# Value matmuls of the transposed score groups by Strassen's method, with score tiles in planned slots

## The chip, the cores and the metric

One Trainium2 chip, one core. The metric is the device time of the whole program in microseconds (us), the median of several executions.

The engines: PE (matmuls), PEld (loads of PE's stationary operand, beside PE), DVE, ACT, POOL, and SP, which only issues transfers here. SPq in a view is SP's transfer queue.

## The reference, cut to what matters

Eight batches of 3008 tokens: an attention with squared relu and a gate, then a feed-forward layer with g = h cos h.

```python
scores = (1.0 / S) * np.matmul(z, z.transpose(0, 2, 1))   # z: 3008 x 64, so scores are symmetric
attn = np.maximum(scores, 0.0) ** 2
x = u * np.matmul(attn, v)                                 # u, v: 3008 x 256
# ... cut: the eight batches laid one after the other, 24064 tokens
h = x @ w_in                                               # 256 -> 2048
g = h * np.cos(h)
y = g @ w_out                                              # 2048 -> 256
```

## The kernel before: the parts that matter

A batch is cut into 6 columns of 512 tokens (the last has 448), a column into 4 blocks of 128. The score group (c, R) is the 512 x 512 piece of columns c and R. Only the groups with R >= c are computed; for R > c the DMA makes a transposed copy, which column R uses later.

```python
# s_squares: relu on ACT, square on DVE, then the transposed copy by the DMA (queue of SP)
nc.scalar.activation(rt[:, i, :], banks[k], AF.Relu)
nc.vector.tensor_tensor(
    t.rearrange("p s k w -> p s k w")[:, 2 * p:2 * p + 2], rv, rv, ALU.mult)
if p == 1:
    fresh[(b, c, R)] = [t[:, :, k, :] for k in range(K)]
    if R > c and not direct(b, R, c):
        tt = tpool.tile([P, K, K, P], FP16, name="tt")
        turned[(b, c, R)] = tt
        nc.sync.dma_start_transpose(
            tt.rearrange("p s k w -> p (s k) w"),
            t.rearrange("p s k w -> p (s k w)"))
# ... cut
# av_chunks: a column's 23 full blocks into two PSUM banks, both halves of v
for nh in range(NDH):
    for n in range(n0, n1):
        j = order[n]
        wn, a = moving(j)                    # a fresh block, or one of a transposed copy
        chain(nc.tensor.matmul(
            acc[nh][:, 0:wn],
            vs(b, j // G)[:, j % G, nh * P:(nh + 1) * P], a,
            start=(n == 0), stop=(n == NJ - 2)))
if n1 == NJ - 1:
    finish()                                 # DVE: x = acc * ut, frees the two banks
# ... cut
# h_quantum: what DVE must do in time, for PE's six other PSUM banks to come free
nc.scalar.activation(c16, hp, AF.Sin, bias=pihalf, scale=inv_s2)
nc.vector.tensor_tensor(gs[(m, ft // FG)][:, ft % FG, :], hp, c16, ALU.mult)
```

Everything is an event at a planned time (8 units a column, about 3.2 us each). `chain` fixes PE's order by these times; a scheduler sets the order of the other engines by when it believes operands to be ready. A *visit* is a bundle of score matmuls with their relus and squares, in the midst of feed-forward work; a visit ends with up to two transposes.

## Time and profile before

| | before |
|---|---|
| time, median of 3 | 1247.27 us (1246.61 to 1248.53) |
| span of the profiled run | 1244.6 us |
| PE busy / idle | 1234.4 / 10.2 us |
| granted clock, mean | 1.000 |
| transposed copy, issue to landing (min / median / max) | 4.3 / 5.4 / 17.6 us |

The prediction below shows the lines themselves. Three habits help with all that follows. First the busy line, for who is full. Then the chain that ended last, for whether the full engine also sets the end. Then single stretches of the timeline, where one line is `start, duration, engine, line, operation, output<-inputs, count, [idle before <-releaser]`.

### The profile page before, as it was taken

How to read it: one execution, taken by the hardware profiler on the slowest of the kernel's cores; microseconds unless marked ns; L12 is line 12 of the kernel's file. 1: busy time of each engine (PE TensorE's matmuls, PEld its weight loads, DVE VectorE, ACT ScalarE, POOL GpSimd, SP SyncE). 2: the span in 40 equal slices, each digit the busy share in tenths (PEclk: the TensorE clock that was granted, in tenths of full speed). 3: DMA queues.
4: the chain of work that ended last, by engine and by line, in shares of the span. 5: the costliest groups of instructions: out<-in, count | busy, mean ns of one | idle time of the engine just before them, and what ended most of it. 6: DMA issues, size and time to landing. Idle time of an engine off the chain costs nothing.

```text
span 1244.6 us, 20404 instructions
## 1 busy us (share of the span) xinstructions
PE 1234.4 (99%) x7533; PEld 680.0 (55%) x7533; DVE 782.0 (63%) x1389; ACT 844.7 (68%) x1609; POOL 145.8 (12%) x201
## 2 busy tenths in 40 slices
PE   9899999999999999999999999999999999999998
PEld 3355555555555555555555555555555555555556
DVE  7766666666666666656666566665666656666555
ACT  6666676666676766667766667766667766667646
POOL 3210101001010010100101011011010111100000
PEclk9999999999999999999999999999999999999999
DMA  9997958679576795757958569685695957957311
GB/s 162 152 174 129 141 91 119 114 122 142 99 117 111 117 144 106 115 111 110 149 101 121 107 109 150 101 129 99 109 158 92 129 101 112 152 101 108 72 33 45
DMA packets 484212, 144.85 MB, mean 116 GB/s; under 512 B 432400, under 2 KB 484112, under 8 KB 484112
## 3 DMA queue, kind: packets, MB, share of 16 engines
q1 hardware_dynamic: 356448, 88.73, 43.1%
q0 software_dynamic: 100400, 29.77, 24.7%
q10 hardware_dynamic: 27264, 25.06, 6.3%
q8 instruction: 59, 0.97, 0.3%
q14 instruction: 41, 0.34, 0.1%
HBM read 60.29 MB, written 24.64 MB: 68 GB/s over the span
## 4 chain that ended last, share of the span: by engine, by line
PE 97%; DMA 2%; DVE 0%; ACT 0%; issue 0%; DVEq 0%; ACTq 0%
PE acc L310 37%; PE w L361 26%; PE w L344 26%; PE w L223 6%; DMA tt<-a 1%; DMA ut<-ust_62 1%; PE acc L285 1%; DMA x<-in_z_dram 0%; DVE g L351 0%; PE w L191 0%; DVE x L331 0%; ACT zT_63 L196 0%; ACT rt L256 0%; DVE a L258 0%; DVE zst L186 0%
## 5 line engine op out<-in xcount | busy, mean ns | idle before, releaser
L361 PE MATMUL w<-w_out_71,g 128*128 128x256 f16 x3008 | 448.6, 273 | 0.0
L344 PE MATMUL w<-x,w_in_70 128*128 128x512 f16 x1504 | 445.6, 379 | 0.8 <-DVE g L351 0.8
L361 PEld LDWEIGHTS <-g 128*128 128x128 f16 x3008 | 294.2, 98 | 191.6 <-issue 1.4
L256 ACT ACTIVATE rt<-w 128x512 f16<-128x512 f32 x489 | 253.1, 613 | 121.2 <-PE w L223 121.2
L258 DVE TENSOR_TENSOR a<-rt 128x1024 f16<-128x1024 f16 x254 | 173.8, 691 | 180.8 <-ACT rt L256 178.3
L344 PEld LDWEIGHTS <-w_in_70 128*128 128x128 f16 x1504 | 147.0, 98 | 59.2 <-issue 3.9
L90 POOL DMA_DIRECT2D ust_62<-in_u_dram x64 | 44.7, 704 | 385.8 <-PE acc L310 355.9
L240 ACT ACTIVATE rt<-w 128x512 f16<-128x512 f32 (+3 forms) x176 | 62.8, 449 | 39.7 <-PE w L223 39.7
L331 DVE TENSOR_TENSOR x<-acc,ut 128x64 f16<-128x64 f32 (+7 forms) x178 | 69.6, 431 | 29.1 <-PE acc L310 26.6
L310 PE MATMUL acc<-a,v_65 128*128 128x512 f16 x336 | 85.8, 380 | 0.0
L310 PEld LDWEIGHTS <-v_66 128*128 128x128 f16 x552 | 51.9, 98 | 61.8 <-issue 14.1
L310 PEld LDWEIGHTS <-v_65 128*128 128x128 f16 x552 | 51.6, 98 | 60.0 <-issue 13.1
L310 PEld LDWEIGHTS <-v_67 128*128 128x128 f16 x552 | 51.9, 98 | 58.7 <-issue 11.1
L310 PEld LDWEIGHTS <-v_68 128*128 128x128 f16 x552 | 51.9, 98 | 57.7 <-issue 10.9
L310 PE MATMUL acc<-a,v_66 128*128 128x512 f16 x312 | 79.4, 379 | 2.6 <-DVE x L331 2.6
L310 PE MATMUL acc<-a,v_68 128*128 128x512 f16 x312 | 79.2, 379 | 0.0
L310 PE MATMUL acc<-a,v_67 128*128 128x512 f16 x312 | 79.1, 379 | 0.0
L368 ACT ACTIVATE ob<-w 128x256 f32<-128x256 f32 x188 | 73.0, 388 | 5.3 <-PE w L361 5.3
L241 DVE TENSOR_TENSOR a<-rt 128x512 f16<-128x512 f16 (+3 forms) x176 | 47.3, 321 | 44.0 <-ACT rt L240 44.0
L90 POOL DMA_DIRECT2D ust_61<-in_u_dram x48 | 36.5, 766 | 224.4 <-PE acc L310 206.7
L310 PE MATMUL acc<-tt,v_68 128*128 128x512 f16 (+1 forms) x240 | 62.2, 371 | 0.0
L310 PE MATMUL acc<-tt,v_67 128*128 128x512 f16 (+1 forms) x240 | 62.1, 371 | 0.0
(1546 smaller groups left out, 1399.8 us busy)
## 6 DMA issues: line engine op xcount, KB each, us to landing
out_dram<-ob ACTq DMA_DIRECT2D x92, 256.0 KB, 2.3
ust_61<-in_u_dram POOLq DMA_DIRECT2D x48, 128.0 KB, 4.0
ust_62<-in_u_dram POOLq DMA_DIRECT2D x32, 128.0 KB, 4.4
a<-a SPq DMA_TRANSPOSE x132, 3.0
v_65<-in_v_dram POOLq DMA_DIRECT2D x4, 512.0 KB, 6.1
v_66<-in_v_dram POOLq DMA_DIRECT2D x4, 512.0 KB, 6.6
v_68<-in_v_dram POOLq DMA_DIRECT2D x4, 512.0 KB, 6.2
v_67<-in_v_dram POOLq DMA_DIRECT2D x4, 512.0 KB, 6.2
```

Of the source, the lines that this page charges most:

```text
L90: hold(nc.gpsimd.dma_start(dst, src))
L223: chain(nc.tensor.matmul(sp[:, s0 * P:], zt[h, R * K + k + 1 - lo, :], zt[h, j0 + s0:j0 + K, :].rearrange("p j w -> p (j w)"), start=True, ...
L240: nc.scalar.activation(rt[:, i, k * P:], banks[k][:, k * P:], AF.Relu)
L241: nc.vector.tensor_tensor(t[:, k, k:, :].rearrange("p s w -> p (s w)"), rt[:, i, k * P:], rt[:, i, k * P:], ALU.mult)
L256: nc.scalar.activation(rt[:, i, :], banks[k], AF.Relu)
L258: nc.vector.tensor_tensor(t.rearrange("p s k w -> p k s w")[:, 2 * p:2 * p + 2], rv, rv, ALU.mult)
L285: chain(nc.tensor.matmul(accs[(b, c)][nh], vs(b, NG - 1)[h, G - 1, nh * P:(nh + 1) * P], a[h], start=False, stop=False))
L310: chain(nc.tensor.matmul(acc[nh][:, 0:wn], vs(b, j // G)[:, j % G, nh * P:(nh + 1) * P], a, start=(n == 0), stop=(n == NJ - 2)))
L331: nc.vector.tensor_tensor(x[:, nh, :], acc[nh][:, o:o + n], ut[:, nh, o:o + n], ALU.mult)
L344: chain(nc.tensor.matmul(hp, w_in16[:, k, ft * P:(ft + 1) * P], x[:, k, :], start=(k == 0), stop=(k == NDH - 1)))
L361: chain(nc.tensor.matmul(ys[m][:, 0:D], gs[(m, f4)][:, ft % FG, ts * P:(ts + 1) * P], w_out16[:, ft, :], start=(ft == 0), stop=(ft == NFT ...
L368: nc.scalar.activation(obs[m][:, i, :], ys[m][:, 0:D], AF.Copy, bias=0.0, scale=inv_s2)
```

## The change

Its intent: PE is full, so do fewer columns of matmul. Four transposed blocks times v are a 2 x 2 product of halves, and Strassen's method (in Winograd's form) needs 7 half products for 8. In columns 2 to 5 up to four transposed groups go this way, 102 groups in all. DVE prepares the sums of scores, POOL the sums of v, ACT and DVE combine the products. The first sums overwrite the transposed copy in place, so score tiles get 18 planned slots instead of two rotating pools of 9 and 13.

```diff
+    slots = [kpool.tile([P, K * CW], FP16, name=f"s{i}") for i in range(NSLOT)]   # NSLOT = 18
-    apool = pool("a", 9)
-    tpool = pool("at", 13)
+    spool = pool("sum", 1)
 ...
+    def v_sums(b, R):                       # POOL, four operations a group (first shown)
+        nc.gpsimd.tensor_tensor(o[:, 0], t[:, k1, d2], t[:, k1, d1], ALU.subtract)
 ...
+    def a_sums1(b, c, R):                   # DVE, reads and writes the transposed copy
+        s1 = quarter(b, c, R, 0, 1)
+        nc.vector.tensor_tensor(s1, s1, quarter(b, c, R, 1, 1), ALU.add)
+        nc.vector.tensor_tensor(
+            second(b, c, R), s1, quarter(b, c, R, 0, 0), ALU.subtract)
+    def a_sums2(b, c, R):                   # DVE, 1024 elements
+        nc.vector.tensor_tensor(dst, src, sub, ALU.subtract)
+    def product(b, c, n):                   # PE: two matmuls of half width a group
+            for k in range(2):
+                chain(nc.tensor.matmul(
+                    acc[bank][:, cols], lhs[:, k, :], rhs[:, k, :], ...))
+    def keep(b, c, n):                      # ACT copies products 1, 5, 7; DVE adds
+        if n in (1, 5):
+            nc.scalar.copy(p15[:, n // 5, 0:h], acc[n // 5][:, h:2 * h])
 ...
+                for i, R in enumerate(W):
+                    at(t - 2.5 + 0.5 * i, 2, lambda b=b, c=c, R=R: a_sums1(b, c, R))
+                    at(t + 1.5 + 0.3 * i, 2, lambda b=b, c=c, R=R: a_sums2(b, c, R))
+                for n, o in ((1, 1.0), (5, 1.0), (2, 1.0), (6, 1.4), (7, 3.0), (3, 3.0), (4, 3.4)):
+                    at(t + o, 2, lambda b=b, c=c, n=n: product(b, c, n))
```

## The prediction

> **What bounds the kernel now.** I read the page's first two parts, then the chain of waits, then the costliest groups, then one stretch of the timeline, then the rows of the transposed score tiles.
>
> ```profile
> PE 1234.4 (99%) x7533; PEld 680.0 (55%) x7533; DVE 782.0 (63%) x1389; ACT 844.7 (68%) x1609; POOL 145.8 (12%) x201
> PEclk9999999999999999999999999999999999999999
> PE acc L310 37%; PE w L361 26%; PE w L344 26%; PE w L223 6%; DMA tt<-a 1%; DMA ut<-ust_62 1%; PE acc L285 1%; DMA x<-in_z_dram 0%; DVE g L351 0%; PE w L191 0%; DVE x L331 0%; ACT zT_63 L196 0%; ACT rt L256 0%; DVE a L258 0%; DVE zst L186 0%
> ```
>
> PE is busy 99% at a full clock, and the chain that ended last is PE for 97%: 37% in the value matmuls (L310) that the change rewrites. The next lines ask whether PE is really streaming, and how late ACT, DVE and the transposes come behind it. Columns of the timeline: start, duration, engine, line, operation, count.
>
> ```profile
> 606.15 0.59 PE L344 MATMUL w<-x,w_in_70 128*128 128x512 f16 x2
> 606.58 0.60 PE L361 MATMUL w<-w_out_71,g 128*128 128x256 f16 x4
> 607.02 0.59 PE L344 MATMUL w<-x,w_in_70 128*128 128x512 f16 x2
> ...
> 610.58 0.82 PE L223 MATMUL w<-zT_63 64*128 64x512 f16 x6
> 611.00 3.04 ACT L256 ACTIVATE rt<-w 128x512 f16<-128x512 f32 x6 [1.52 <-PE w L223]
> ...
> 612.84 5.49 SPq L265 DMA_TRANSPOSE tt<-a  x2
> ...
> 613.88 0.73 ACT L348 ACTIVATE c_7345<-w,pihalf 128x512 f16<-128x512 f32 x1
> ...
> 616.24 0.38 ACT L368 ACTIVATE ob<-w 128x256 f32<-128x256 f32 x1
> ```
> ```profile
> DMA to landing us min/median/max: 4.3/5.4/17.6
> ```
>
> Starts: two 512-column matmuls take 0.43 us, four 256-column ones 0.44 us, so PE loses nothing and halving a matmul's width costs almost nothing. There is no waiting to remove: only columns. After a visit of six score matmuls (610.58) ACT needs 3.0 us for its six relus, works through four sines until 616.2 and then the output copy: 6.0 us behind the visit. And a tile that the DMA transposes lands 4.3 us after its issue at best, 5.4 in the median (last fence, the rows of tile tt). Today only PE reads it, much later, so nobody cares.
>
> **What the Trainium skill says.** (1) "TensorE: Matmul & The Clock Gate", section "Wait — 56ns, not 53.3ns?": a matmul takes N/2.4 GHz plus about 2.5 ns. The trace agrees: starts lie 216 ns apart at 512 columns, 109 at 256, 189 at 448. (2) "PSUM — Partial Sum Buffer", section "PSUM bank collisions raise a hardware error": two engines must not touch one bank at once, so an accesses' order must be guarded by bank. The trace of before has no such case; in the built order of after, the copy of product 1 does wait for product 2, which writes the other half of that bank. (3) The same page, "Engine vs sequencer instructions": ScalarE and VectorE queues are strict FIFO. The trace's DVE order is exactly the built order, all 1389 instructions. (4) "VectorE: DVE Perf Modes", section "The perf-mode tier table": 16-bit tensor_tensor runs at two elements a cycle, with a PSUM operand at one. The trace agrees: 691 ns for 1024 elements of L258, 416 ns for 256 from PSUM (L331).
>
> **The change part by part.**
>
> PE. A full transposed group was 4 blocks x 2 halves = 8 matmuls of 512 columns, 8 x 0.2158 = 1.727 us. It becomes 7 products x 2 = 14 of 256, 14 x 0.1092 = 1.528 us: 0.198 saved. In column 5 (448 wide): 8 x 0.1892 - 14 x 0.0958 = 0.172. Groups: columns 2, 3, 4 have 2+3+4 in each of batches 1 to 7, and 3+4 in batch 0: 70; column 5 has 4 x 8 = 32. Saved: 70 x 0.198 + 32 x 0.172 = **19.4 us**. Everything on PE saved would give 1247.3 - 19.4 = 1227.9. That is 1.6%, so a gain over 2% is out of reach.
>
> DVE. Per group two sums of 512 elements (423 ns each, row L241) and one of 1024 (691): 1.54 us, x 102 = 157. Per Strassen column (31 of them) two of 256 from PSUM (0.416) and one of 512 (0.68): 1.5, x 31 = 47. DVE goes from 782 to about 985 us, 79% of the span. ACT: 3 copies of 0.38 x 31 = 35, to 880. POOL: 128 sums of v, in column 0, a column and more before use. None of these becomes a bound by itself. What counts is where PE must wait in order. I counted that in the built order, batch by batch (batches 1 to 7 have the same pattern), against the times above.
>
> - Columns 3 and 4: product 6 follows product 2 with nothing between, and waits for the ACT copy that waits for product 2. Last matmul of product 2 starts at s; ACT starts at s + 0.27 (its duration) + 0.04 (the visit: 610.58 + 0.38, the mean of a 512-column matmul, to 611.00), copies 0.38, PE answers 0.05 later: s + 0.74, where s + 0.11 was due. 0.63 us each, 16 times, and once in column 5 of batch 7, which has no score visit: 17 x 0.63 = **10.7 us**.
> - Column 2: a score visit fills that gap, but product 4 comes due 5.5 us after the visit, and its ACT copy stands behind six relus, four sines and an output copy (6.0 us) + 0.38 + 0.05. 0.9 us, 7 times: **6 us**. In column 5 the products are longer, and it fits.
> - The first activation sums of each group stand in the DVE queue right behind the squares that made the group, because the scheduler moved them far forward of their place in the text. Each needs the transposed tile. DVE blocks until it lands, 4.3 to 5.4 us after the squares (2 us more for the second of a visit), where the next DVE work, the product g, is due 2 to 4 us earlier. PE waits wherever it needs a PSUM bank that a late g, or a late finish of a column, frees. Per batch I find: before column 5 (second of a visit, finish late) 1.0 to 1.3; at the wrap to column 0 (same) 1.4 to 2.0; column 1, where the last score matmul needs the g behind the blocked sum, 0.4 to 1.4; three smaller places, 0.5 to 1.2 together. 3.3 to 5.9 us a batch, x 7 = **23 to 41 us**.
>
> Sum: 1247.3 - 19.4 + 10.7 + 6 + (23 to 41) = 1268 to 1286.
>
> **The rivals.**
>
> *All of the saving arrives* (1228). For it: PE is the bound everywhere, and DVE and ACT have a third of the span free. Against: PE has no idle time to absorb a wait, and the waits of product 6 on ACT are certain in the order. It needs zero cost at 17 + 7 places.
>
> *Only the ACT round trips cost* (1247.3 - 19.4 + 16.7 = 1245, level). This is the case if the six PSUM banks and the buffers let PE run on while DVE is blocked. For it: in the timeline g ends about 1 us before the score matmul that needs its bank, so part of each block is swallowed; and a wait of PE in one place gives DVE time for the next, so my sum counts some twice. Against: the blocks are 2 to 3 us and the slack 1.
>
> *DVE blocked on transposes sets the pace* (1268 to 1286, the sum above). For it: landing times of 4.3 us at best, a strict FIFO, a built order that puts the sum there 13 times a batch. Were the transposes slower under more traffic (maximum 17.6), it would be above 1290.
>
> *The planned slots (18 for 22 buffers) add waits of their own.* The SP and DVE waits on PE in the order are for matmuls long past; I give it nothing.
>
> **Range and chances.** I trust the ACT waits (16.7 us) most, and take the DVE ones at about half of the middle of their range, 32, for the double counting: -19.4 + 16.7 + about 19 = +16, or **1264 us**. The low end, 1232, is all of the saving with a few of the waits; the high end, 1288, is the full sum. Over 2% faster is 1222.8, below what all columns saved can give: 0.01. Over 2% slower begins at 1272.2, inside my sum of the third rival: 0.35. Within 2%: 0.64.
>
> **What will show it.** PE busy time must fall by about 19 us and the value lines must show 1428 matmuls of 224 and 256 columns at 96 and 109 ns from start to start; if these run slower, the first term is wrong. The waits must list PE behind the ACT copies about 24 times, 0.6 to 0.9 us each. DVE must show idle time before the first sums (a_sums1), released by the transposes, some 1 to 3 us each and about 100 times; PE must then show waits on g and on the finish of a column, together 20 to 40 us. If DVE waits there but PE shows no wait on DVE, the second rival holds; if DVE does not wait, my reading of the order is wrong and the time is near 1240. If PE waits for v sums on POOL or for slots, I missed a term.

## The result, and the profile after

**1407.04 us** (median of 4, 1401.65 to 1409.64). The ratio to the kernel before is 1.1278, with a 95% interval of 1.1252 to 1.1304. A ratio here is the mean time of one kernel's fast runs over the mean of the other's fast runs of the same rounds, so it is not quite the ratio of the medians.

From the page of the kernel after: the busy line, PE's busy digits, the granted clock, and the chain by engine.

```profile
PE 1272.8 (90%) x8145; PEld 752.0 (53%) x8145; DVE 955.0 (68%) x1788; ACT 885.3 (63%) x1702; POOL 234.6 (17%) x329
...
PE   6689799997999879998799987999879898899999
...
PEclk8799999998999989999999999999999999999999
...
PE 70%; DMA 16%; DVE 6%; ACT 4%; issue 3%; ACTq 0%; DVEq 0%; SPq 0%
```

PE has fewer columns to do and yet is busy *longer*, 1272.8 for 1234.4 us. It is also idle for 1407.9 - 1272.8 = 135.1 us, where it was 10.2 before. Its busy digits dip to 7 with a rhythm, about every five slices of 35 us: once a batch. The chain that ended last, 97% PE before, now leads for 16% through DMAs. That is the first sign of the cause: not an engine that is full (DVE is at 68%), but transfers that someone stands and waits for.

Next the waits of the kernel after, `engine, output, line <- what ended the wait: total us, times, longest`. L376 is the first sum of a group (the in-place add of `a_sums1`), L458 the product g, L347 the finish of a column, L236 the score matmuls, L419 the Strassen products, L439 and L432 the ACT copies of products.

```profile
DVE s L376 <- DMA s<-s: 199.5, 72, 7.8
...
ACT c L455 <- DVE g L458: 84.9, 57, 7.1
...
PE w L236 <- DVE g L458: 46.8, 17, 7.0
...
PE acc L419 <- DVE x L347: 37.5, 13, 5.3
...
PE acc L324 <- DVE x L347: 10.4, 2, 7.4
...
PE acc L419 <- ACT q L439: 9.4, 14, 0.9
...
PE acc L419 <- ACT p L432: 8.2, 17, 0.8
```

Read it downwards as one chain. DVE stands 199.5 us before the first sums, until a transposed copy lands. Behind it in DVE's queue are g and the finish of a column, so ACT and PE wait for these: PE for 46.8 + 37.5 + 10.4 = 94.7 us. The waits of PE on ACT, which the prediction trusted most, are there too, 31 times, but only 17.6 us together. One more wait is left out here: 12.8 us of PE on a relu of DVE (L267), 8.9 of them in one piece at the start; e2 and e5 come to it.

One such place in the timeline of the kernel after. The visit is at 510 us; the two transposes are issued at 512.44 and 516.5.

```profile
512.44 8.23 SPq L278 DMA_TRANSPOSE s<-s  x2
...
513.68 0.69 DVE L271 TENSOR_TENSOR s<-rt 128x1024 f16<-128x1024 f16 x1 [0.29 <-ACT rt L269]
...
514.29 1.28 DVE L458 TENSOR_TENSOR g<-w,c 128x512 f16<-128x512 f32 x2
...
516.35 0.44 PE L236 MATMUL w<-zT 64*128 64x512 f16 x3
...
520.54 0.94 DVE L376 TENSOR_TENSOR s<-s 128x512 f16<-128x512 f16 x1 [4.98 <-DMA s<-s]
...
521.40 1.27 DVE L458 TENSOR_TENSOR g<-w,c 128x512 f16<-128x512 f32 x2
522.13 1.18 PE L236 MATMUL w<-zT 64*128 64x256 f16 x3 [5.35 <-DVE g L458]
...
524.07 1.06 PE L451 MATMUL w<-x,w_in 128*128 128x512 f16 x2
```

The first copy lands at 520.45, 8.0 us after its issue. Until then DVE does nothing, although sines for g are ready. Six PSUM banks fill up; PE issues three score matmuls and stops. Only after 4.98 us does the sum run, then g, and then PE, which has stood for 5.35 us. The last line holds a second loss: two matmuls of 512 columns take 1.06 us, where the same pair took 0.59 in the kernel before.

Windows of 1 us of the kernel after, with busy time (and instructions) of PE, PEld, DVE, ACT and POOL, then the granted clock, DMA share and GB/s:

```profile
526.00:527.00 1.00, 1.00 (x4) 0.46 (x3) 0.98 (x2) 0.12 (x1) 0.00 (x0) 0.50 1.38 216
527.00:528.00 1.00, 1.00 (x6) 0.55 (x4) 0.40 (x1) 0.56 (x1) 0.00 (x0) 0.66 0.44 86
528.00:529.00 1.00, 1.00 (x9) 0.69 (x8) 0.35 (x2) 0.69 (x1) 0.00 (x0) 1.00 0.00 0
```

From 522 to about 527.7 the clock is 0.50 (the mean of 0.66 in the second window holds both rates), so PE is "busy" and does half the work: a wait of 5.35 us costs about 8, by an estimate from these numbers (5.35 and half of 5.5). The Trainium skill, page "TensorE: Matmul & The Clock Gate", Part 1: The HAM clock gate, says that PE runs at half rate after an idle window of about 3.4 us and returns to full after a window of sustained work. The trace agrees in kind (0.50, then 1.00); its lengths differ, as the last section tells.

This makes the batch from 489.40 to 661.15 us 171.75 us long, where a batch of the kernel before takes about 154.5 (its transposes of one place in the batch start at 568.74 and 723.21). Its PE is idle for 12.8 us: 4.2 and 5.35 in two places behind late copies, 2.0 in three waits on ACT, and small ones.

### The profile page after: what moved, and what is told of

Read it like the earlier page. It is cut to its first block, busy times and chain, and to the rows that moved or that the text cites. A ratio compares the mean times of both kernels' runs of the same rounds, so it can differ in the third digit from the quotient of the medians.

```text
span 1407.9 us, 22304 instructions
## 1 busy us (share of the span) xinstructions
PE 1272.8 (90%) x8145; PEld 752.0 (53%) x8145; DVE 955.0 (68%) x1788; ACT 885.3 (63%) x1702; POOL 234.6 (17%) x329
## 4 chain that ended last, share of the span: by engine, by line
PE 70%; DMA 16%; DVE 6%; ACT 4%; issue 3%; ACTq 0%; DVEq 0%; SPq 0%
PE w L468 18%; PE w L451 18%; PE acc L324 18%; DMA s<-s 16%; PE acc L419 10%; PE w L236 5%; ACT rt L269 2%; DVE g L458 2%; DVE x L347 1%; DVE s L271 1%; DVE s L391 1%; DVE s L376 1%; PE acc L298 1%; ACT c L455 1%; ACT p L432 0%
## 5 line engine op out<-in xcount | busy, mean ns | idle before, releaser
L455 ACT ACTIVATE c<-w,pihalf 128x512 f16<-128x512 f32 x752 | 502.0, 704 | 300.7 <-PE w L451 209.9
L458 DVE TENSOR_TENSOR g<-w,c 128x512 f16<-128x512 f32 x752 | 491.2, 685 | 89.3 <-ACT c L455 86.1
L468 PE MATMUL w<-w_out,g 128*128 128x256 f16 x3008 | 453.1, 274 | 0.0
L451 PE MATMUL w<-x,w_in 128*128 128x512 f16 x1504 | 452.1, 384 | 0.0
L324 PE MATMUL acc<-s,v 128*128 128x512 f16 (+1 forms) x1392 | 345.2, 386 | 10.4 <-DVE x L347 10.4
L271 DVE TENSOR_TENSOR s<-rt 128x1024 f16<-128x1024 f16 x254 | 187.3, 743 | 113.7 <-ACT rt L269 113.5
L324 PEld LDWEIGHTS <-v 128*128 128x128 f16 x1392 | 130.2, 99 | 177.0 <-issue 64.6
L376 DVE TENSOR_TENSOR s<-s 128x512 f16<-128x512 f16 (+1 forms) x102 | 43.7, 429 | 199.6 <-DMA s<-s 199.5
L451 PEld LDWEIGHTS <-w_in 128*128 128x128 f16 x1504 | 149.0, 99 | 52.9 <-issue 6.7
L236 PE MATMUL w<-zT 64*128 64x512 f16 (+3 forms) x684 | 109.9, 374 | 63.3 <-DVE g L458 46.8
L419 PE MATMUL acc<-s,vsum 128*128 128x256 f16 (+1 forms) x816 | 112.5, 279 | 19.5 <-ACT q L439 9.4
L419 PE MATMUL acc<-s,v 128*128 128x256 f16 (+1 forms) x612 | 87.2, 286 | 37.5 <-DVE x L347 37.5
L419 PEld LDWEIGHTS <-vsum 128*128 128x128 f16 x816 | 79.7, 101 | 51.1 <-issue 42.9
L419 PEld LDWEIGHTS <-v 128*128 128x128 f16 x612 | 62.6, 104 | 48.6 <-DVE x L347 37.3
L236 PEld LDWEIGHTS <-zT 64*128 64x128 f16 x684 | 26.0, 95 | 113.3 <-issue 100.6
L347 DVE TENSOR_TENSOR x<-acc,ut 128x64 f16<-128x64 f32 (+7 forms) x178 | 68.9, 431 | 3.6 <-PE acc L324 3.5
```

The costliest lines, as they stand in the source:

```text
L236: chain(nc.tensor.matmul(sp[:, s0 * P:], zt[h, R * K + k + 1 - lo, :], zt[h, j0 + s0:j0 + K, :].rearrange("p j w -> p (j w)"), start=True, ...
L271: nc.vector.tensor_tensor(t.rearrange("p s k w -> p k s w")[:, 2 * p:2 * p + 2], rv, rv, ALU.mult)
L324: chain(nc.tensor.matmul(acc[nh][:, 0:wn], vs(b, j // G)[:, j % G, nh * P:(nh + 1) * P], a, start=(start and n == 0), stop=(last and n == ...
L347: nc.vector.tensor_tensor(x[:, nh, :], acc[nh][:, o:o + n], ut[:, nh, o:o + n], ALU.mult)
L419: chain(nc.tensor.matmul(acc[bank][:, cols], lhs[:, k, :], rhs[:, k, :], start=(n in (1, 5) and i == k == 0), stop=(i == len(W) - 1 and k ...
L451: chain(nc.tensor.matmul(hp, w_in16[:, k, ft * P:(ft + 1) * P], x[:, k, :], start=(k == 0), stop=(k == NDH - 1)))
```

## The experiments

Eleven kernels ran, all correct. "Gain" compares medians.

| kernel | median us | range | ratio to before (95%) |
|---|---|---|---|
| e1: slots alone | 1244.42 | 1243.79 to 1248.26 | 0.9996 (0.9974 to 1.0018) |
| e2: after, first sums late | 1272.33 | 1270.67 to 1273.88 | 1.0217 (1.0193 to 1.0241) |
| e3: before + an early idle sum | 1360.25 | 1358.55 to 1367.41 | 1.0930 (1.0896 to 1.0964) |
| e4: before + a late idle sum | 1266.57 | 1264.77 to 1272.95 | 1.0177 (1.0145 to 1.0208) |
| e5: e2 + sums of v paced | 1254.78 | 1251.44 to 1256.17 | 1.0064 (1.0044 to 1.0085) |
| e6: e5 + products reordered | **1237.41** | 1236.35 to 1238.22 | **0.9931** (0.9914 to 0.9948) |
| e7: e6, first sums early again | 1368.10 | 1365.78 to 1372.09 | 1.0985 (1.0957 to 1.1013) |
| e8: after, 2 of 13 sums late | 1358.16 | 1356.45 to 1362.39 | 1.0900 (1.0875 to 1.0925) |
| e9: after, the other 11 late | 1339.18 | 1335.50 to 1340.90 | 1.0738 (1.0715 to 1.0762) |
| e10: after, 3 of 13 late | 1311.59 | 1309.73 to 1314.73 | 1.0533 (1.0509 to 1.0558) |
| e11: after, one v load later | 1402.43 | 1396.90 to 1405.20 | 1.1238 (1.1208 to 1.1269) |

### e1: the slots alone

```diff
-    NW = 4
+    NW = 0
```

> The changed kernel with Strassen switched off in every column (NW = 0): the planned slots stay, all value matmuls are full ones again. Theory A (the loss is DVE blocked on freshly issued transposes): there are no sums, so the time is that of before, 1247 us within 5, with PE at 99% and a clock of 1.00. Rival C (18 planned slots in place of 22 rotating buffers make score tiles wait): over 1270 us.

Measured 1244.42 us, ratio 0.9996. No Strassen, 18 slots: as fast as before. The slots cost nothing, and the fourth rival is out.

### e2: the first sums behind the last g

The sums stay what they are. Each first sum only gets an order (no wait on a semaphore) behind the last g issued before it in the text, so it stands where its text stands.

```diff
-        nc.vector.tensor_tensor(s1, s1, quarter(b, c, R, 1, 1), ALU.add)
+        add = nc.vector.tensor_tensor(s1, s1, quarter(b, c, R, 1, 1), ALU.add)
+        if lastg:
+            after(add.ins, lastg[0], NOSYNC)
 ...
-        nc.vector.tensor_tensor(gs[(m, ft // FG)][:, ft % FG, :], hp, c16, ALU.mult)
+        g = nc.vector.tensor_tensor(gs[(m, ft // FG)][:, ft % FG, :], hp, c16, ALU.mult)
+        lastg[:] = [g.ins]
```

> The changed kernel, with one thing more: the first activation sum of a group may not be moved ahead of the last g product issued before it in the text, so it stands in the DVE queue where the text has it, a column or more after its transpose was issued. Same work on every engine. Theory A: DVE's 200 us of waiting on transposes ends, PE no longer waits on g or on the finish of a column, the clock is 1.00, and what is left is -19 us of columns and about +17 us of round trips over ACT: 1240 to 1255 us. Rival B (the amount of new work on DVE and ACT, or the ACT round trips, set the pace): over 1340 us.

Measured 1272.33 us: 134.7 us come back, for an order alone. The time is still above the expected 1240 to 1255. The clock is 0.996. DVE's wait for transposes is gone from the sixty longest; what is left, from the waits of e2 (L421, L441, L434 are the products and the two ACT copies):

```profile
PE acc L421 <- ACT q L441: 17.8, 14, 1.3
...
PE w L236 <- DVE zT L201: 8.8, 1, 8.8
...
PE acc L421 <- ACT p L434: 8.4, 17, 1.1
```

So 26.2 us of waits on ACT, where the prediction had 16.7, and one single wait of 8.8 us that it had not at all. That one is at the start, in the timeline of e2:

```profile
11.12 0.69 POOL L358 TENSOR_TENSOR vsum<-v 128x256 f16<-128x256 f16 x1
...
11.54 10.61 DVE L271 TENSOR_TENSOR s<-rt 128x1024 f16<-128x1024 f16 x2
...
20.61 1.00 POOL L361 TENSOR_TENSOR vsum<-v,vsum 128x256 f16<-128x256 f16 x1
...
22.82 1.03 PE L236 MATMUL w<-zT 64*128 64x512 f16 x4 [8.79 <-DVE zT L201]
```

Two squares of DVE, 0.69 us each elsewhere, last 10.6 us: about as long as POOL's sixteen sums of v, which run back to back for 10.5 us. The Trainium skill, page "SBUF — State Buffer", section "Who interferes with whom", says that a DVE instruction with two SBUF inputs contends with a POOL instruction that reads SBUF. The trace agrees, and here the pair of squares lasted through all sixteen instructions of POOL. It isn't always so: at 301.44 us of the same run a square of 512 elements, started among eight such sums, took 0.96 us, where the same square took 0.42 us in the kernel before.

### e3 and e4: an idle sum in the kernel before, early and late

Does the mechanism need Strassen at all? The kernel before gets one DVE sum of 512 elements per transposed copy, into a scrap tile that no one reads. In e3 the scheduler places it, right behind the squares; in e4 it is issued 3.7 units later and held behind the last g.

```diff
+    scrap = kpool.tile([P, K, P], FP16, name="scrap")
 ...
+                probe = nc.vector.tensor_tensor(              # e3, after the transpose
+                    scrap, tt[:, 0, :, :], tt[:, 1, :, :], ALU.add)
 ...
+        op = nc.vector.tensor_tensor(scrap, tt[:, 0, :, :], tt[:, 1, :, :], ALU.add)   # e4
+        if lastg:
+            after(op.ins, lastg[0], NOSYNC)
 ...
+                at(t + 3.7, 2, lambda b=b, c=c, R=R: probe(b, c, R))
```

> The kernel before, with one idle DVE sum of 512 elements per transposed score tile that reads the tile and writes a scrap tile; the scheduler puts it right behind the squares, as it does with the sums of the change. 117 ops of 0.42 us are 49 us of DVE work, which DVE (63% busy) could hide. Theory A: DVE blocks on each landing as in the changed kernel, and the time goes to 1340 to 1420 us without any Strassen. Rival B: at most 1260 us.

Measured 1360.25 us, 113 us more than before, for 117 operations that give nothing and add 36.9 us to DVE's busy time. From its waits (L354 is g there, L334 the finish):

```profile
DVE scrap L269 <- DMA tt<-a: 232.0, 114, 6.5
...
PE w L224 <- DVE g L354: 40.0, 25, 6.3
...
PE acc L313 <- DVE x L334: 35.2, 14, 11.6
```

The same three lines as in the changed kernel. The early place of an operation that needs a transposed copy is enough.

> The same as the run before it, but the idle DVE sum is issued 3.7 time units (about 12 us) after the score visit and held behind the last g product. Same work, no wait. Theory A: 1247 us within 6, no DVE idle time released by a transpose. Rival B (any 49 us more of DVE work costs, wherever it stands): the same time as with the early sum.

Measured 1266.57 us: most of it is gone, but it should have been level. A wait `DVE scrap L272 <- DMA tt<-a` of 41.4 us in 17 places remains: 19.3 us of it, in 7 places, in the first 100 us, the rest later. What PE loses lies in these first 100 us, in batch 0, where there is hardly a g behind which to hold a sum (the first runs at 68.3 us). Windows of e4, then of the kernel before:

```profile
25.00:50.00 25.00, 14.55 (x66) 4.72 (x64) 14.14 (x24) 8.61 (x17) 1.40 (x2) 0.80 1.03 146
50.00:75.00 25.00, 20.48 (x88) 7.01 (x87) 18.25 (x32) 14.06 (x27) 7.97 (x11) 0.88 1.17 134
100.00:125.00 25.00, 25.00 (x155) 13.56 (x154) 15.41 (x30) 17.43 (x36) 2.40 (x3) 1.00 0.70 115
```
```profile
25.00:50.00 25.00, 22.37 (x118) 7.63 (x116) 20.02 (x32) 14.28 (x28) 4.38 (x6) 1.00 1.30 146
50.00:75.00 25.00, 23.67 (x121) 10.27 (x118) 19.55 (x34) 20.98 (x40) 6.89 (x9) 1.00 1.62 160
```

PE loses 7.8 + 3.2 us there, and runs at a clock of 0.80 and 0.88 on top; from 100 to 175 us it is full. My expectation missed, then, most likely because the edit did not hold the sums where no g was; no run shows that alone.

### e5: the sums of v paced

e2, and each of POOL's sums of v held behind the PE matmul before it in the text, half a unit apart, in batch 0 from unit 12 on.

```diff
-    def v_sums(b, R):
+    def v_sums(b, R, k):                     # one of the four
+        hold(nc.gpsimd.tensor_tensor(*args, ALU.subtract))
 ...
+            for k in range(4):
+                at(b * span + (2.0 if b else 12.0) + 0.5 * (4 * R + k), 2,
+                   lambda b=b, R=R, k=k: v_sums(b, R, k))
```

> The late-sums kernel, with each of the sums of v on POOL held behind the PE matmul that stands before it in the text, so that the 16 of a batch are spread over some 30 us. In the late-sums run the 16 of batch 0 ran back to back from 11 to 21 us, and one DVE square of 0.69 us took 9.5 us over just that time. Theory A2 (that square was blocked by POOL reading SBUF, and PE with it): no DVE square over 2 us, PE's wait of 9 us at the start gone, 1259 to 1265 us. Rival (the stretch at the start waits for something else, a load): 1272 us still.

Measured 1254.78 us: 17.5 us gained, more than expected. The block of 10 us at the start is gone (the same squares take 1.29 us a pair), and PE's waits on the second ACT copy fell from 17.8 to 9.7 us. Why the copies came earlier, once POOL was paced, I did not test.

### e6: the products in another order

e5, and product 2 moved behind product 6 in columns 3 and 4, product 4 later in columns 2 and 5, so that other matmuls lie between a product and the copy that it waits for.

```diff
-                for n, o in ((1, 1.0), (5, 1.0), (2, 1.0), (6, 1.4), (7, 3.0), (3, 3.0), (4, 3.4)):
+                for n, o in ((1, 1.0), (5, 1.0), (2, 1.41 if c in (3, 4) else 1.0), (6, 1.4),
+                             (7, 3.0), (3, 3.0), (4, 5.0 if c in (2, 5) else 3.4)):
```

> The run before it, with two moves in the order of the products: in columns 3 and 4 product 2 goes behind product 6, so that the copy of product 1 no longer waits for product 2; in columns 2 and 5 product 4 (with the first value chunk of column 2) goes behind the next four h and y groups, so that its ACT copy has 3.5 us more. Theory A3 (what is left over the pure column time is the round trips over ACT, 4.1 us a batch in the late-sums run): the PE waits on ACT copies fall from 26 us to under 4, and the time to 1230 to 1240 us, below the kernel before. Rival (these waits are replaced by others, DVE being 77% busy): 1255 us or more.

Measured 1237.41 us, ratio 0.9931: **faster than both kernels**, by 0.7% than the one before. The interval (0.9914 to 0.9948) leaves 1 out. From its page and its waits:

```profile
PE 1217.6 (99%) x8145; PEld 739.2 (60%) x8145; DVE 946.9 (77%) x1788; ACT 876.0 (71%) x1702; POOL 241.5 (20%) x329
...
PE acc L422 <- ACT p L435: 3.1, 9, 0.9
PE acc L422 <- DVE s L394: 3.0, 10, 0.8
```

PE is busy 16.8 us less than before, of the 19.4 that the columns were to save, and 6.1 us of waits in the products are left. The narrow matmuls run as fast as predicted: eight of 224 columns take 0.77 us (573.52 to 574.29), 96 ns each. The saving of Strassen's method is real; it is only small.

### e7: the first sums early again

e6 without the three lines of e2 that hold the first sum.

```diff
-        add = nc.vector.tensor_tensor(s1, s1, quarter(b, c, R, 1, 1), ALU.add)
-        if lastg:
-            after(add.ins, lastg[0], NOSYNC)
+        nc.vector.tensor_tensor(s1, s1, quarter(b, c, R, 1, 1), ALU.add)
```

> The version with paced v sums and reordered products, but with the first sums where the scheduler of the changed kernel puts them, right behind the squares. Theory A (DVE blocked on transposes that have not landed carries the loss on its own, whatever else is mended): 1237 + 135 = about 1370 us, 1345 to 1390, with DVE idle of 150 to 200 us before the first sums and a granted clock of about 0.96. Rival (the blocks only hurt together with the starting POOL block and the products' waits on ACT): 1250 to 1290.

Measured 1368.10 us, 130.7 us above e6, at a clock of 0.965. From its waits:

```profile
DVE s L377 <- DMA s<-s: 183.7, 72, 7.2
```

The early sums cost about the same with everything else mended as with nothing mended (134.7; the 4.0 us between lie inside the ranges of the runs). So this term doesn't depend on the other two and may be added to them.

### e8, e9, e10: which of the 13 first sums of a batch

The hold of e2 only for some of the groups (named by the two columns that they join). e8 holds (0,2) and (0,4), e9 the other eleven, e10 holds (0,2), (0,4) and (0,5).

```diff
+        if lastg and (c, R) in ((2, 0), (4, 0)):               # e8
+        if lastg and (c, R) not in ((2, 0), (4, 0)):           # e9
+        if lastg and (c, R) in ((2, 0), (4, 0), (5, 0)):       # e10
+            after(add.ins, lastg[0], NOSYNC)
```

> The changed kernel, where only two of the 13 first sums of a batch are held behind the last g: those of transposed groups (0,2) and (0,4), which in the batch that I read took 11.7 of the 24.3 us that DVE waited for transposes, and stood before 9.6 of the 12.1 us that PE lost. Theory A1 (a few late landings around the change of batch, where the v loads share the DMA engines, carry most of the loss): 1290 to 1325 us, a gain of 80 to 115 of the 135 us. Rival A2 (the place is not special: once these two are gone, the same blocks bite at the next sums): 1335 to 1390.

> The counterpart: the other eleven first sums of each batch held, the two of groups (0,2) and (0,4) left where the changed kernel has them. Theory A1: 1350 to 1385 us, little gained. Rival A2: 1285 to 1330.

Measured 1358.16 and 1339.18 us: e8 gained 48.9 us and e9 67.9. The first lies in A2's range, the second in neither. Left alone (e9), the two sums still cost 66.9 us over e2, half of the loss. Timeline of e8:

```profile
490.52 8.95 SPq L278 DMA_TRANSPOSE s<-s  x2
...
501.47 0.39 DVE L376 TENSOR_TENSOR s<-s 128x448 f16<-128x448 f16 x1 [6.63 <-DMA s<-s]
...
503.55 1.86 PE L324 MATMUL acc<-s,v 128*128 128x512 f16 x4 [4.27 <-DVE x L347]
```

The sum of (0,4) is held, and that of (0,5), 448 wide and from the *same visit*, now stands at the head of DVE's queue and waits longer, since its copy is issued after the other. So I ran e10.

> The changed kernel with three first sums a batch held: groups (0,2), (0,4) and (0,5). In the run with two held, the sum of (0,5), made in the same visit as (0,4), took over its wait: 6.63 us for DVE and 4.27 us for PE at the same place. Theory A1 mended (two visits around the change of batch carry most of the loss, and a visit's wait goes away only when both of its sums are held): 1358 - 7 batches x (4.3 idle + about 3 of slow clock) = about 1307, 1290 to 1320. Rival A2 (whatever is mended, the next sum takes over): 1335 to 1358.

Measured 1311.59 us, clock 0.990: three sums out of 13, in two visits, carry 95.5 of the 134.7 us (71%). DVE still waits 102.1 us for transposes, in 51 places, but PE's waits on the finish and on g are down from 94.7 to 8.5 + 6.0 + 3.6 us. Short waits of DVE are mostly swallowed; the long ones hit PE.

### e11: a load of v moved away

Why are the copies around the change of batch late? At 509.80 us POOL issues a load of 512 KB of v, 2.6 us before the transposes. e11 issues it next to the following load.

```diff
-                at(t + (-1.5, -0.4, -0.1)[g] * U, 0, lambda b=b, g=g: load_v(b, g))
+                at(t + (-1.5, -0.12, -0.1)[g] * U, 0, lambda b=b, g=g: load_v(b, g))
```

> The changed kernel with one load of v a batch (512 KB, the second group, issued 2.7 us before the transposes of the visit that makes groups (0,4) and (0,5), which then took 8.0 and 6.2 us to land) moved 7 us later, next to the third. Theory A3 (that load is what makes these transposes late): they land after 4.5 to 6 us, the first sum of (0,4) waits about 2 to 3 us less, and at 7 batches the time falls by 20 to 45 us, to 1362 to 1387. Rival (the transposes are late because of the two loads of u, of each other, or of the moved load's new place): 1395 to 1415, with landings as before.

Measured 1402.43 us: no gain clear of the noise (the two intervals overlap), the rival's range. From the timeline of e11, the sums of (0,4) and (0,5):

```profile
514.50 0.42 DVE L376 TENSOR_TENSOR s<-s 128x512 f16<-128x512 f16 x1 [3.04 <-DMA s<-s]
521.26 0.39 DVE L376 TENSOR_TENSOR s<-s 128x448 f16<-128x448 f16 x1 [5.13 <-DMA s<-s]
```

The first copy came earlier (a wait of 3.04 us for 4.98), the second later: it landed 10.8 us after its issue, beside the load at its new place (POOL issues it at 512.6). The late landing went with the load; the wait only changed hands. That transposes and loads slow one another is consistent with this and not proven by it: the visit that makes (0,2), with landings of 7.8 and 8.5 us, runs beside two loads of u, which I did not move.

## Why the prediction was wrong

The direction and the third rival's mechanism were right, the size was not: 1264 predicted with 1232 to 1288 around it, 1407 measured; and a loss of over 2% had been given a chance of only 0.35. By its terms, each measured by the experiment that takes it away:

| term | predicted | measured | by |
|---|---|---|---|
| columns saved on PE | -19.4 | -16.8 in PE's busy time; -8.6 in the time of e6 (by the ratio), with waits of 6.1 left | e6 against before |
| waits of products on ACT | +16.7 | 17.4 gained by reordering (26.2 in the waits of e2) | e6 against e5 |
| POOL | 0 | 17.5 | e5 against e2 |
| DVE blocked on transposes | about +19, of 23 to 41 | **134.7**, and again 130.7 | e2 against after, e7 against e6 |
| slots | 0 | 0 (ratio 0.9996) | e1 |

The waits on POOL and on ACT were each taken away in one order only (after the block of DVE), so these two sizes hold for that order.

- **Columns saved: right**, nearly. That PE's busy time rose in the changed kernel did not refute it, because a half clock counts as busy; only runs at full clock could show it. The last 2.6 us are not explained; e5 and e6, with the same matmuls at a clock of 1.000, differ by 4.6 us in busy time (1222.2 and 1217.6), so they are within what this measure can tell.
- **Waits on ACT: right in place and count** (24 predicted, 31 seen).
- **POOL: a missed term.** The prediction counted POOL's sums as work "a column and more before use" and asked when they end, not what they block meanwhile.
- **DVE blocked: the step that failed.** The prediction's own check, "some 1 to 3 us each and about 100 times" of DVE before the first sums, came out as 72 waits of 2.8 us. Its next check, waits of PE on g and finish, "together 20 to 40 us", came out as 94.7. So the block was sized well and its passing on was not. Three things went wrong there:
  1. The sum used the *median* landing, 5.4 us, though the maximum of 17.6 stood in the same line. At the places that the prediction had named, "before column 5" and "at the wrap to column 0", the copies took 8.5 and 8.0 us, and PE lost 4.2 and 5.35 us in place of 1.0 to 1.3 and 1.4 to 2.0. The prediction had itself said that slower transposes would take it above 1290, but did not look how late they were at these places. The trace of the kernel before shows it: in the batch from 568.74 us on, the four copies of these two visits (known by their place among the 15 of a batch) landed 9.0, 8.7, 9.8 and 10.2 us after their issue, the other eleven after 4.3 to 6.3.
  2. The sum was then halved "for the double counting" (half of 32 is 16; "about 19" is a slip of 3 us). The measured 94.7 us lie above even the whole sum of 23 to 41, so halving led away from it; and by e10, 71% of the loss goes with three sums, in the two visits with the latest copies.
  3. It had no term for the clock. Between after and e2 the profiled spans differ by 138.9 us. 89.9 of this is PE's idle time (135.1 against 45.2) and 49.0 is busy time (1272.8 against 1223.8) for the same matmuls. The clock is the visible reason for the 49.0 (0.959 against 0.996), but no run changed the clock alone.

## What to carry to other kernels

An operation that needs a transfer belongs in a strict queue where the transfer has surely landed, not where a scheduler believes it ready: here an order without any wait was worth 134.7 us. Size such a block by the longest landing at that very place, and add the time that PE then runs at half clock. And a saving of 1.6% on the full engine leaves so little room that every helper (copies, sums, even on an idle engine) must be placed by hand before it pays: e6 kept 0.7%.

## What the Trainium skill lacked or had wrong

- "TensorE: Matmul & The Clock Gate", Part 1: The HAM clock gate: the idle window of about 3.4 us is not a safe limit. In e11 a gap of 2.90 us (PE back at 515.59) was followed by a clock of 0.53 and 0.50 from 517 to past 520, 1.4 us *after* PE had work again (but for one more gap of 0.20 us); a gap of 2.79 us shortly after was followed by none. After gaps of 4.21 and 5.35 us in the changed kernel the half rate lasted about 3.1 and 5.5 us after PE's restart.
- "SBUF — State Buffer", section "Who interferes with whom": it doesn't say over how many instructions of the other engine such a wait can last. In e2 DVE's pair of squares lasted 10.6 us, through POOL's whole run of sixteen sums of 0.66 to 1.00 us; at 301.44 us of the same run a square waited about one sum (0.96 us for 0.42).
- No page says how long a transposed copy takes from issue to landing beside other transfers (it would belong to "DMA: Bandwidth & Descriptors"): 4.3 us at best for 128 x 2048 elements of 16 bits in the kernel before, 8.0 and 8.5 us at the change of batch in the changed kernel, 10.8 us in e11. Nor that SP's issue of one such transpose itself takes about 4 us there (3.96 and 4.18 us for the pair at 512.44, where the quickest of the kernel takes 1.32), so that the second of a pair starts that much later.
